# Memory updates in column tiles and memory reads in row tiles, with a new order of the work

## The chip, the cores and the metric

The kernel runs on one core of a Trainium2 chip. A core has TensorE (matmuls, "PE" in the profile, with its weight loads as "PEld"), VectorE ("DVE"), ScalarE ("ACT"), GpSimd ("POOL") and SyncE ("SP", which here issues nearly all DMAs). TensorE reads SBUF and writes PSUM, which has 8 banks; a bank holds 128 partitions x 512 floats. The metric is the device time of one execution in microseconds.

## The reference

Four layers work on x of 2048 tokens x 512 channels: attention with a compressive memory, a GEGLU feed-forward network, and both once more with the same weights. All inputs are bf16.

```python
x = x + A(layernorm(x));  x = x + B(layernorm(x))      # twice

def A(x):                       # 32 heads of 16 channels; 4 segments of 512 tokens
    q, k, v = split(x @ wq), split(x @ wk), split(x @ wv)
    phi = lambda t: where(t > 0, t + 1, exp(t))
    M, z = 0, 0                 # per head: 16 x 16 and 16
    for s in range(4):
        a_dot = softmax(qs @ ks.T / 4 + causal mask) @ vs
        a_mem = (phi(qs) @ M) / (phi(qs) @ z + 1e-6)
        o_s = sigmoid(beta) * a_mem + (1 - sigmoid(beta)) * a_dot
        M, z = M + phi(ks).T @ vs, z + sum(phi(ks))
    return concat(o) @ wo

def B(x):                       # 1792 hidden channels
    return (gelu(x @ w_gate) * (x @ w_up)) @ w_down
```

## The kernel before

**Stages.** The two attention layers with their four segments make eight attention segments, `Att(k)`, k = 0 to 7, and the two feed-forward layers eight `Ffn(k)`. Segment k of attention is followed by segment k of the feed-forward network; segments of different k overlap. Channels of q, k and v are in four blocks of 128 (b = 0 to 3), each with eight heads of 16 channels.

**TensorE's work.** Dense products (q, k, v, wo, gate, up, down) go through `product` (L399-409): a 128x128 weight tile against 512 columns. If the array is already split, the product is issued as four matmuls with 32 weight columns each ("columns", L406); otherwise as one ("whole", L409). Scores (`score_round`, L832) split the array by rows: four matmuls of four heads run beside each other ("rows"), each into another PSUM bank. `flush_item` (L848), which multiplies the exponentials with v, uses columns. `Clocks.tiling` marks each change between whole, rows and columns.

**The exponentials.** One ScalarE instruction (L1256) takes a pair of PSUM banks; GpSimd then zeroes the part above the diagonal (L1262). 320 such pairs make up the score work.

**The memory.** For every segment that is not the last of its layer, `upd_item` computes phi(k).T @ v: for each of four token tiles j and each block b one whole matmul of 128x128 weights with 128 columns (L758), 16 an update. Of the 128x128 results only the 16x16 blocks on the diagonal belong to a head, so VectorE masks them with `bd` into `mblk` (L770) and keeps a sum in `macc` (L785, L787); the sums z go into `zcols` (L774). The state is `mblk` (128 columns a block) and `zcols` (8 columns a block). For every segment that is not the first, `mem_items` reads it: 16 matmuls of 8 columns give the denominators (L681), VectorE adds the epsilon, multiplies with the gate and inverts (L688, L693), then for each block four matmuls of 128 columns give the numerators (L704), and VectorE scales one bank of 512 columns (L714) into `am`. `turn_later` has SP's queue transpose `am` into `amT` by DMA, and VectorE adds `amT` to the softmax part `aT` (L881). There are six updates and six reads in the program.

**What sets the order.** All five engines' instructions are written out by hand, in the order that `order` finds when the program is built: it keeps a clock for each engine, with a cost for each operation, and a list of `items` with due times, and at each step lets TensorE take score rounds first (`rounds_now`), then go on with an item that is open, then open the ready item that is due first, if a PSUM bank is free (`pick`). If nothing is ready while scores remain, TensorE multiplies a constant tile ("warm", a filler). Due times and slacks are in `POLICY`. The order is fixed in the program; on the chip the engines wait for each other by semaphores.

Of the kernel before, what the change touches and what calls it, by code (L numbers as in the profile page):

```python
# [18 lines left out]
P = 128  # L19
# [11 lines left out]
VW = H * (DH + 1)  # L31
SCALE = DH ** -0.5
# [12 lines left out]
def narrow(pieces, par):  # L45
# [19 lines left out]
    flush_wait=31.24, piece_slack=21.809, kb_slack=10.712, mem_slack=-1.256, margin=2.578, qk_due=1.366,  # L65
    e_q=-0.208, e_k=1.104, exp_slack=-8.673, e_slack=10.49, phi_slack=11.84, gelu_slack=-0.257, act_evict=7.504,
    first_evict=-5.126, gate_step=0.0, up_due=1.343, up_step=0.018, down_due=3.044, down_step=0.196,
    upd_due=-0.283, v0_due=-0.631, x1_at=2.428, x2_at=1.735, x3_at=6.651, x3_load=17.614, cut_slack=-5.505,
    direct=4, gelu_tiles=1, phi_pool=0, kb_dve=5, rounds=2, early=8.837, starve=0.645, ahead=0.994, near=-6.896,
    cap=1, soon=6.003)  # L70
# [187 lines left out]
def order(pol, nc, cst, seg, wrk, psp, A_x, A_wq, A_wk, A_wv, A_wo, A_beta, B_x, B_w_gate, B_w_up, B_w_down, out):  # L258
# [79 lines left out]
    maskB = cst.tile([P, 1], F32, name="maskB")  # L338
    nc.vector.reduce_sum(out=maskB[:], in_=bd[:, 16:P:32], axis=mybir.AxisListType.X)
# [4 lines left out]
    macc = cst.tile([P, 4, P], F32, name="macc")  # L344
# [11 lines left out]


    def later_constants():
        def column(va):
            nc.vector.tensor_copy(out=by_head(va)[:, :, :, DH], in_=cden[:].unsqueeze(1).to_broadcast([P, TPS, H]))  # L360
            nc.vector.memset(va[:, :, VW:], 0.0)

        for n, va in enumerate(vaugs[-1:] + vaugs[:-1]):
            ck.dve.post(12.0 + 3.0 * n, NORMAL, (0.4, lambda va=va: column(va), None))

# [148 lines left out]
    items = []  # L514
    e_jobs = []
# [4 lines left out]
    class Att:  # L520
# [12 lines left out]
        def add_items(self):  # L533
# [32 lines left out]
            def k_done(b, ps, at=None):  # L566
# [4 lines left out]
                def told(t):  # L571
# [5 lines left out]
                    if k < pol.kb_dve:  # L577
                        ck.dve.post(t, pol.kb_slack if k else NORMAL, (Slowed(0.345, 0.06), lambda: nc.vector.tensor_scalar(  # L578
                            out=self.kB[:, b, :], in0=self.kf[:, b, :], scalar1=maskB[:, 0:1], scalar2=None,
                            op0=ALU.mult), lambda t2: ev.update({("kB", k, b): t2})))  # L580
# [88 lines left out]
        def mem_items(self):  # L669
            k = self.k  # L670

            def ready(*more):
                return ck.has(*[("phiq", k, b) for b in range(4)], ("mem", k - 1), *more)

            den = Psum()

            def dens():
                return den()[:, 0:TPS * H].rearrange("p (j b h) -> p j b h", b=4, h=8)

            def den_mm(j, b):  # L680
                nc.tensor.matmul(dens()[:, j, b, :], lhsT=self.phiq[:, b, j * P:(j + 1) * P],  # L681
                                 rhs=mem_state[k - 1][1][:, b, :], start=True, stop=True)

            def den_done():
                def add():
                    self.rdm = wrk.tile([P, TPS, 4, 8], F32, tag="rdm", bufs=1, name="rdm")

                    nc.vector.scalar_tensor_tensor(  # L688
                        out=self.rdm[:], in0=dens(), scalar=EPS_MEM, op0=ALU.add, op1=ALU.mult,
                        in1=tmp_e2[:].rearrange("p (b h) -> p b h", h=8).unsqueeze(1).to_broadcast([P, TPS, 4, 8]))  # L690

                ck.dve.post(ck.made(), NORMAL, (0.273, add, den.read),
                            (0.956, lambda: nc.vector.reciprocal(out=self.rdm[:], in_=self.rdm[:]),  # L693
                             lambda t: ev.update({("den", k): t})))

            items.append(Item(k + 0.01, lambda: ready() and (self.s == 1 or ("am", k - 1) in ev),
                              [(Clocks.SMALL, whole(lambda j=j, b=b: den_mm(j, b))) for j in range(TPS) for b in range(4)],
                              den_done, kind="mem", ps=den, after=("phiq", k, 3)))

            def num(b):  # L700
                ps = Psum()

                def mm(j):
                    nc.tensor.matmul(ps()[:, j * P:(j + 1) * P], lhsT=self.phiq[:, b, j * P:(j + 1) * P],  # L704
                                     rhs=mem_state[k - 1][0][:, b, :], start=True, stop=True)

                def done():
                    self.n_num += 1
                    if self.n_num == 4:
                        ev["memn", k] = ck.pe  # L710

                    def scale():
                        self.am = seg.tile([P, TPS, P], BF16, tag=f"am{b % 2}", bufs=1, name="am")
                        nc.vector.tensor_tensor(  # L714
                            out=self.am[:].rearrange("p t (h e) -> p t h e", e=DH),
                            in0=ps()[:].rearrange("p (t h e) -> p t h e", h=8, e=DH),
                            in1=self.rdm[:, :, b, :].unsqueeze(3).to_broadcast([P, TPS, 8, DH]),
                            op=ALU.mult)

                    def told(t):  # L720
                        ps.read(t)
                        am = self.am
                        self.n_am += 1
                        if self.n_am == 4:
                            ev["am", k] = t
                        self.amT[b] = seg.tile([P, L], BF16, tag=f"amT{b}", bufs=1, name="amT")
                        turn_later(t, NORMAL, lambda: self.amT[b][:].rearrange("p (t q) -> p t q", q=P),
                                   lambda: am[:].rearrange("p t d -> p (t d)"),
                                   lambda t2: ck.at(t2 + 1.0, lambda: ev.update({("amT", k, b): t2 + 1.0})))

                    ck.dve.post(ck.made(), NORMAL, (0.683, scale, told))

                def go():
                    return (ready(("den", k)) and (b < 2 or ("amT", k, b - 2) in ev)
                            and (self.s == 1 or (("amT", k - 1, (b + 2) % 4 if b < 2 else b) in ev
                                                 and ("aT", k - 1, b) in ev)))

                return Item(k + 0.02 + 0.001 * b, go, [(Clocks.MM[128], whole(lambda j=j: mm(j))) for j in range(TPS)], done,
                            kind="mem", ps=ps, after=("den", k))

            for b in range(4):
                items.append(num(b))

        def upd_item(self):
# [3 lines left out]
            def blocks():  # L748
                return psm().rearrange("p (b d) -> p b d", d=P)
# [6 lines left out]
            def m(c):  # L756
                j, b = divmod(c, 4)
                nc.tensor.matmul(blocks()[:, b, :], lhsT=self.phik[:, j, b * P:(b + 1) * P],  # L758
                                 rhs=by_head(self.vaug)[:, j, 8 * b:8 * b + 8, 0:DH], start=(c == 0), stop=(c == n_mm - 1))

            def done():
# [3 lines left out]
                def kept(t):  # L765
                    made.append(seg.tile([P, 4, P], BF16, tag=f"mblk{k % 2}", bufs=1, name="mblk"))
                    made.append(seg.tile([P, 4, 8], BF16, tag=f"zcols{k % 2}", bufs=1, name="zcols"))

                def gated(src):
                    return lambda: nc.vector.tensor_tensor(out=made[0][:], in0=src(),  # L770
                                                           in1=bd[:].unsqueeze(1).to_broadcast([P, 4, P]), op=ALU.mult)

                def z():
                    nc.vector.tensor_tensor(out=made[1][:], in0=bd[:, 0:P:16].unsqueeze(1).to_broadcast([P, 4, 8]),  # L774
                                            in1=zacc[:].unsqueeze(2).to_broadcast([P, 4, 8]), op=ALU.mult)
# [5 lines left out]
                if self.s == 0:  # L781
                    steps = [(0.154, lambda: nc.vector.tensor_copy(out=zacc[:], in_=self.zk[:]), kept),
                             (0.683, gated(blocks), None),
                             (0.2, z, told),
                             (0.683, lambda: nc.vector.tensor_copy(out=macc[:], in_=blocks()), psm.read)]  # L785
                else:
                    steps = [(0.683, lambda: nc.vector.tensor_tensor(out=macc[:], in0=macc[:], in1=blocks(),  # L787
                                                                     op=ALU.add), psm.read),
                             (0.154, lambda: nc.vector.tensor_tensor(out=zacc[:], in0=zacc[:], in1=self.zk[:],
                                                                     op=ALU.add), kept),  # L790
                             (0.683, gated(lambda: macc[:]), None),
                             (0.2, z, told)]
                ck.dve.chain(ck.made(), pol.mem_slack, *steps)

            items.append(Item(k + pol.upd_due, ready, [(Clocks.MM[128], whole(lambda c=c: m(c))) for c in range(n_mm)],
# [406 lines left out]

    def open_item(got, bank):
# [85 lines left out]
    while streams or items or opened or ck.busy():  # L1289
        assert ck.pe < 2000.0, (streams[:1], [(it.kind, it.due) for it in items[:9]], e_jobs[:2], banks)  # L1290
        ck.serve()
        next_e()
# [92 lines left out]
```

## Time and profile before

| | before |
|---|---|
| median of 3 runs | 555.61 us (555.18 to 556.28) |
| span of the profiled execution | 553.5 us (first to last instruction; its device time as a whole isn't listed, the runs' times stand for it) |
| TensorE busy | 545.0 us, 98% |
| VectorE busy | 450.1 us, 81% |
| ScalarE busy | 445.3 us, 80% |
| GpSimd busy | 281.2 us, 51% |
| granted TensorE clock | 1.000 |

"Busy" of TensorE is the time in which some matmul is under way. Matmuls are pipelined, so a matmul's own duration is longer than the distance to the next. In the views of groups a row is: source line, engine, operation, out<-in, tile of the array and shapes, count, then busy time and mean duration in ns, then the engine's idle time before these instructions and what ended it. In the view of waits a row is: who waited, for whom, us in total, times, longest. The view in order of time has the start, the length and the group. Where a group of matmuls holds several shapes, the view in order of time names the first.

### The profile page before, as it was taken

How to read it: one execution, taken by the hardware profiler on the slowest of the kernel's cores; microseconds unless marked ns; L12 is line 12 of the kernel's file. 1: busy time of each engine (PE TensorE's matmuls, PEld its weight loads, DVE VectorE, ACT ScalarE, POOL GpSimd, SP SyncE). 2: the span in 40 equal slices, each digit the busy share in tenths (PEclk: the TensorE clock that was granted, in tenths of full speed). 3: DMA queues.
4: the chain of work that ended last, by engine and by line, in shares of the span. 5: the costliest groups of instructions: out<-in, count | busy, mean ns of one | idle time of the engine just before them, and what ended most of it. 6: DMA issues, size and time to landing. Idle time of an engine off the chain costs nothing.

```text
span 553.5 us, 22415 instructions
## 1 busy us (share of the span) xinstructions
PE 545.0 (98%) x9769; PEld 271.6 (49%) x9769; DVE 450.1 (81%) x837; ACT 445.3 (80%) x570; POOL 281.2 (51%) x410
## 2 busy tenths in 40 slices
PE   8999999999999999999999999999999999999997
PEld 4444554444544445444445445444554446455544
DVE  7999999879978999689896888968978696876062
ACT  5899999999999898999999899999539987930500
POOL 2687766268617878237882356836427264300000
PEclk9999999999999999999999999999999999999999
DMA  8246602500231032302142021031321006100001
GB/s 263 45 105 141 180 3 41 165 11 3 31 58 22 12 48 54 60 2 41 22 59 41 4 47 34 12 41 22 57 62 31 2 4 98 21 2 21 19 2 39
DMA packets 66467, 26.63 MB, mean 48 GB/s; under 512 B 55104, under 2 KB 66368, under 8 KB 66368
## 3 DMA queue, kind: packets, MB, share of 16 engines
q1 hardware_dynamic: 65936, 24.92, 21.7%
q8 instruction: 76, 1.25, 0.9%
q10 hardware_dynamic: 432, 0.27, 0.2%
q14 instruction: 23, 0.19, 0.1%
HBM read 9.71 MB, written 2.10 MB: 21 GB/s over the span
## 4 chain that ended last, share of the span: by engine, by line
PE 82%; DVE 13%; DMA 2%; issue 1%; ACT 0%; POOL 0%; DVEq 0%
PE ps L406 43%; PE ps L409 22%; PE ps L832 8%; PE ps L848 5%; DVE st L435 2%; DVE xn L465 1%; DVE byq L863 1%; DMA phik<-e 1%; DVE x_sb L918 1%; PE ps L704 1%; PE ps L758 1%; DVE vaug L396 1%; DVE q L396 1%; DVE ab L871 1%; DVE kB L578 1%
## 5 line engine op out<-in xcount | busy, mean ns | idle before, releaser
L1256 ACT ACTIVATE pt<-ps 128x1024 bf16<-128x1024 f32 x320 | 309.4, 1025 | 42.9 <-PE ps L832 32.5
L1262 POOL TENSOR_SCALAR_AFFINE_SELECT pt<-pt 128x512 bf16<-128x512 bf16 (+1 forms) x320 | 186.3, 589 | 182.2 <-ACT pt L1256 179.6
L978 DVE TENSOR_TENSOR gel_sb<-gel_sb,ps 128x512 bf16<-128x512 bf16 x112 | 76.4, 687 | 47.2 <-PE ps L406 27.8
L653 POOL TENSOR_SCALAR e<-e 128x512 bf16<-128x512 bf16 x48 | 74.2, 1546 | 4.7 <-ACT e L635 2.2
L406 PE MATMUL ps<-xnT,wu_sb 128*32 128x512 bf16 x1280 | 73.6, 379 | 0.0
L406 PE MATMUL ps<-xnT,wg_sb 128*32 128x512 bf16 x1144 | 68.9, 380 | 0.3 <-DVE x_sb L918 0.3
L918 DVE TENSOR_TENSOR x_sb<-x_sb,ps 128x512 bf16<-128x512 bf16 (+1 forms) x68 | 43.0, 643 | 24.6 <-PE ps L409 16.3
L406 PE MATMUL ps<-wd_sb,gel_sb 128*32 128x512 bf16 (+1 forms) x1060 | 60.5, 369 | 0.0
L863 DVE STREAM_TRANSPOSE byq<-ps 128x512 f32<-128x512 f32 x64 | 45.0, 705 | 6.7 <-PE ps L848 6.5
L406 PEld LDWEIGHTS <-wu_sb 128*32 128x32 bf16 x1280 | 33.0, 97 | 33.2 <-issue 2.8
L409 PE MATMUL ps<-wd_sb,gel_sb 128*128 128x512 bf16 (+1 forms) x239 | 45.1, 342 | 0.0
L406 PEld LDWEIGHTS <-wg_sb 128*32 128x32 bf16 x1144 | 28.9, 96 | 28.5 <-issue 5.5
L848 PE MATMUL ps<-pt,vaug 128*32 128x256 bf16 (+2 forms) x1568 | 40.8, 243 | 0.4 <-ACT gel_sb L956 0.3
L435 DVE BATCH_NORM_STATS2 st<-x_sb 128x6 f32<-128x512 bf16 x60 | 40.5, 674 | 0.2
L1030 ACT ACTIVATE gel_sb<-gel_sb 128x512 bf16<-128x512 bf16 x70 | 38.4, 628 | 0.1
L406 PEld LDWEIGHTS <-gel_sb 128*32 128x32 bf16 x1060 | 26.0, 96 | 24.1 <-issue 4.6
L409 PE MATMUL ps<-xnT,wg_sb 128*128 128x512 bf16 x162 | 37.7, 379 | 0.0
L848 PEld LDWEIGHTS <-vaug 128*32 128x32 bf16 x1568 | 31.9, 97 | 10.5 <-issue 2.9
L396 DVE CAST gel_sb<-ps 128x512 bf16<-128x512 f32 x46 | 30.8, 682 | 5.1 <-PE ps L406 4.7
L465 DVE TENSOR_SCALAR xn<-x_sb,mv,rs 128x512 bf16<-128x512 bf16 x64 | 30.7, 534 | 1.2 <-POOL rs L453 0.9
L832 PE MATMUL ps<-q,kf 16*128 16x256 bf16 (+1 forms) x896 | 31.1, 232 | 0.2 <-DVE vaug L396 0.2
L409 PEld LDWEIGHTS <-gel_sb 128*128 128x128 bf16 x239 | 22.6, 98 | 17.0
(129 smaller groups left out, 739.0 us busy)
## 6 DMA issues: line engine op xcount, KB each, us to landing
wg_sb<-in_B_w_gate_dram SPq DMA_DIRECT2D x8, 224.0 KB, 3.6
wu_sb<-in_B_w_up_dram SPq DMA_DIRECT2D x8, 224.0 KB, 4.6
wd_sb<-in_B_w_down_dram SPq DMA_DIRECT2D x7, 256.0 KB, 3.2
x_sb<-in_A_x_dram SPq DMA_DIRECT2D x3, 512.0 KB, 8.0
out_dram<-x_sb SPq DMA_DIRECT2D x12, 128.0 KB, 1.8
xnT<-xn SPq DMA_TRANSPOSE x48, 2.5
kB<-kf SPq DMA_DIRECT2D x48, 16.0 KB, 1.8
wv_sb<-in_A_wv_dram SPq DMA_DIRECT2D x1, 512.0 KB, 7.1
```

Source lines behind the costliest of these rows:

```text
L396: ck.dve.post(ck.made(), slack, (0.673, lambda: nc.vector.tensor_copy(out=dst(), in_=src()), end), taken=taken)
L406: nc.tensor.matmul(out[r], lhsT=lhsT[:, r], rhs=rhs, start=start, stop=stop, tile_position=(0, 32 * c))
L409: nc.tensor.matmul(out, lhsT=lhsT, rhs=rhs, start=start, stop=stop)
L435: nc.vector.bn_stats(out=self.st6[:, 0, :], in_=x_sb[:, self.tt0 + j, :])
L653: return lambda: eng.tensor_scalar(out=e[0][:], in0=e[0][:], scalar1=1.0, scalar2=None, op0=ALU.min)
L832: nc.tensor.matmul(ps_all[:, pair[unit // 2], o:o + n], lhsT=lhsT[rows, b, P * ki:P * ki + P], rhs=self.q[rows, b, q0:q0 + n], start=True, ...
L848: nc.tensor.matmul(ps()[32 * j:32 * j + 32, q0:q0 + n], lhsT=self.vaug[:, ki, h * (DH + 1):h * (DH + 1) + 32], rhs=pt_all[:, slot, unit, c ...
L863: nc.vector.transpose(out=self.byq[:, par, :, :].rearrange("p a c -> p (a c)"), in_=ps()[:])
L918: ck.dve.post(ck.made(), slack, (0.15 + 0.00104 * (c1 - c0), lambda: nc.vector.tensor_tensor(out=xt, in0=xt, in1=ps()[:, 0:c1 - c0], op=AL ...
L978: ck.dve.post(ck.made(), NORMAL, (0.683, lambda: nc.vector.tensor_tensor(out=g, in0=g, in1=ps()[:], op=ALU.mult), lambda t: (ps.read(t), e ...
L1256: nc.scalar.activation(out=pt_all[:, s0, :, :].rearrange("p (h u) c -> p h (u c)", h=2), in_=ps_all[:, p0[0]:p0[1] + 1, :], func=ACT.Exp, ...
L1262: nc.gpsimd.affine_select(out=half, in_=half, pattern=[[0, w], [1, P]], compare_op=ALU.is_ge, fill=0.0, base=0, channel_multiplier=-1)
```

## The change

The state of the memory becomes one tile `mz` with 34 columns a block: two heads of 16 columns and one column of z each. The update is issued in four column tiles: for each token tile and block four matmuls with 32 weight columns (two heads) and 32 columns of v. So each result has only 32 columns, of which two 16x16 blocks are kept, and VectorE's steps on it have 128 elements in place of 512. The read is issued in four row tiles: 32 rows of phi(q) (two heads) against 34 columns of `mz`, into four banks, denominators beside numerators. It works on half of the blocks at a time (`mem_event`), as a single block of 32 matmuls, and no longer through `items`: `mem_now` starts it when its inputs are there and two pairs of banks are free. VectorE then has per half two additions (32 elements), one reciprocal (64) and four scalings (256), with the gate laid out in a new constant `e2x`. The values of `POLICY` are others, so that the whole order of the work is new; `kb_dve` goes from 5 to 4 (the copy kB of the keys is made by DMA for one more segment) and `direct` from 4 to 5 (one more of each segment's 14 gate tiles goes through GELU straight from PSUM).

```diff
+MZ = 2 * DH + 2
 POLICY = dict(
-    flush_wait=31.24, piece_slack=21.809, ..., kb_dve=5, ..., direct=4, ...)
+    flush_wait=152.105, piece_slack=40.738, ..., kb_dve=4, ..., direct=5, ..., am_slack=1.081, mem_wait=0.156)
...
-    maskB = cst.tile([P, 1], F32, name="maskB")
-    nc.vector.reduce_sum(out=maskB[:], in_=bd[:, 16:P:32], axis=mybir.AxisListType.X)
+    mask2 = cst.tile([P, 2 * DH], F32, name="mask2")
+    nc.vector.reduce_sum(out=mask2[:], in_=bd[:].rearrange("p (c n) -> p n c", c=4), axis=mybir.AxisListType.X)
...
-    macc = cst.tile([P, 4, P], F32, name="macc")
+    macc = cst.tile([P, 4, 2 * DH], F32, name="macc")
+    e2x = cst.tile([P, 2, 2, 2, 4 * TPS], F32, name="e2x")
...
         def mem_items(self):
-            ...  (den_mm, den_done, num: one item for the denominators, four for the numerators)
+            for half in range(2):
+                mem_jobs.append((self.k + 0.01 + 0.002 * half, self, half))
+
+        def mem_event(self, half, pairs):
+            k, bs = self.k, (2 * half, 2 * half + 1)
+            ck.tiling("rows")
+            mz = mem_state[k - 1][0]
+            for n in range(2 * TPS):
+                b, j = bs[n // TPS], n % TPS
+                for g in range(4):
+                    r = slice(32 * g, 32 * g + 32)
+                    nc.tensor.matmul(ps_all[:, pairs[g // 2][g % 2], MZ * n:MZ * (n + 1)],
+                                     lhsT=self.phiq[r, b, j * P:(j + 1) * P], rhs=mz[r, b, :], start=True, stop=True,
+                                     tile_position=(32 * g, 0))
+            ...
+            ck.dve.post(ck.made(), pol.am_slack, (0.16, add(0), None), (0.16, add(1), None), (0.52, inverse, None),
+                        (0.78, scale(0), lambda t: read(0, t)), (0.78, scale(1), told))
...
         def upd_item(self):
             def m(c):
                 j, b = divmod(c, 4)
-                nc.tensor.matmul(blocks()[:, b, :], lhsT=self.phik[:, j, b * P:(b + 1) * P],
-                                 rhs=by_head(self.vaug)[:, j, 8 * b:8 * b + 8, 0:DH], start=(c == 0), stop=(c == n_mm - 1))
+                ck.tiling("columns")
+                for g in range(4):
+                    r = slice(32 * g, 32 * g + 32)
+                    nc.tensor.matmul(blocks()[r, b, :], lhsT=self.phik[:, j, b * P + 32 * g:b * P + 32 * g + 32],
+                                     rhs=by_head(self.vaug)[:, j, 8 * b + 2 * g:8 * b + 2 * g + 2, 0:DH], start=(c == 0),
+                                     stop=(c == n_mm - 1), tile_position=(0, 32 * g))
...
+    def mem_now():
+        if not mem_jobs or len(free_pairs()) < 2:
+            return False
+        got = [j for j in mem_jobs if j[1].mem_ready(j[2])]
+        ...
+        job[1].mem_event(job[2], pairs)
+        return True
...
         ck.serve()
         next_e()
+        if mem_now():
+            continue
         n = rounds_now()
```

More of the change, by code (lines that the diff above doesn't have):

```diff
@@ L64 @@
 POLICY = dict(
[L65 to L70, printed above, removed]
+    flush_wait=152.105, piece_slack=40.738, kb_slack=10.905, mem_slack=-2.348, margin=2.56, qk_due=0.594,
+    e_q=-0.77, e_k=1.073, exp_slack=-18.49, e_slack=11.096, phi_slack=6.459, gelu_slack=-0.034, act_evict=5.372,
+    first_evict=-0.382, gate_step=0.0, up_due=1.256, up_step=0.012, down_due=3.948, down_step=1.013,
+    upd_due=-0.62, v0_due=1.254, x1_at=0.158, x2_at=5.744, x3_at=0.964, x3_load=17.129, cut_slack=-0.231,
+    direct=5, gelu_tiles=1, phi_pool=0, kb_dve=4, rounds=2, early=0.939, starve=0.658, ahead=0.286, near=-3.652,
+    cap=7, soon=1.448, am_slack=1.081, mem_wait=0.156)
 class Slowed(float):
@@ L355, in gate_constants, with gate_rows @@
         nc.vector.tensor_scalar(out=tmp_e2[:], in0=tmp_e2[:], scalar1=1.0, scalar2=None, op0=ALU.add)
+    def gate_rows(half, b):
+        for p in range(2):
+            nc.vector.tensor_copy(
+                out=e2x[:, half, p, :, 2 * TPS * b:2 * TPS * (b + 1)].rearrange("p g (j h) -> p g j h", h=2),
+                in_=tmp_e2[:].rearrange("p (a b q g h) -> p a b q g h", a=2, b=2, q=2, g=2)[:, half, b, p, :, :]
+                .unsqueeze(2).to_broadcast([P, 2, TPS, 2]))
     def later_constants():
@@ L364, in later_constants @@
             ck.dve.post(12.0 + 3.0 * n, NORMAL, (0.4, lambda va=va: column(va), None))
+        for n in range(4):
+            ck.dve.post(26.0 + 2.0 * n, NORMAL, (0.25, lambda n=n: gate_rows(*divmod(n, 2)), None))
     def turn_later(t, slack, out, in_, landed, margin=0.0):
@@ L669, in mem_items @@
         def mem_items(self):
[L670 to L739, printed above, removed]
@@ L741, in mem_items, with mem_ready @@
-            for b in range(4):
-                items.append(num(b))
+            for half in range(2):
+                mem_jobs.append((self.k + 0.01 + 0.002 * half, self, half))
+        def mem_ready(self, half):
+            k, s, bs = self.k, self.s, (2 * half, 2 * half + 1)
+            return (ck.has(*[("phiq", k, b) for b in bs], by=ck.pe - 0.055) and ck.has(("mem", k - 1), by=ck.pe - 0.055)
+                    and (s == 1 or all(("amT", k - 1, b) in ev and ("aT", k - 1, b) in ev for b in bs)))
@@ L1201, in pick @@
         return min(got, key=lambda i: (-len(pairs_of(set(range(BANKS)) - {i, *apart})), banks[i]))
+    def mem_now():
+        if not mem_jobs or len(free_pairs()) < 2:
+            return False
+        got = [j for j in mem_jobs if j[1].mem_ready(j[2])]
+        if not got or (ck.mode != "rows" and streams and min(got)[0] > streams[0][0] + streams[0][1] / STEPS + pol.mem_wait):
+            return False
+        job = min(got, key=lambda j: j[0])
+        mem_jobs.remove(job)
+        pairs = sorted(free_pairs(), key=lambda p: max(banks[p[0]], banks[p[1]]))[:2]
+        job[1].mem_event(job[2], pairs)
+        return True
     def open_item(got, bank):
@@ L1287, in order @@
     owner = defaultdict(list)
-    while streams or items or opened or ck.busy():
+    while streams or items or mem_jobs or opened or ck.busy():
         assert ck.pe < 2000.0, (streams[:1], [(it.kind, it.due) for it in items[:9]], e_jobs[:2], banks)
```

75 lines of the change are left out of this document (59 added, 16 removed).

## The prediction

> **What bounds the kernel now.** I read the page first (span, busy shares, chain), then the waits, then stretches of the span, then TensorE's instructions in order of time, because a busy share cannot say what one instruction costs.
>
> ```profile
> span 553.5 us, 22415 instructions
> PE 545.0 (98%) x9769; PEld 271.6 (49%) x9769; DVE 450.1 (81%) x837; ACT 445.3 (80%) x570; POOL 281.2 (51%) x410
> ...
> PE 82%; DVE 13%; DMA 2%; issue 1%; ACT 0%; POOL 0%; DVEq 0%
> ```
> ```profile
> 28.00:165.00 137.00, 134.61 (x2510) 66.44 (x2510) 126.04 (x237) 129.34 (x164) 88.38 (x123) 1.00 0.33 74
> 165.00:390.00 225.00, 224.08 (x4420) 109.19 (x4421) 192.07 (x349) 210.23 (x265) 139.12 (x195) 1.00 0.19 32
> ...
> 490.00:553.50 63.50, 59.99 (x540) 31.20 (x532) 28.71 (x51) 9.55 (x16) 1.27 (x2) 1.00 0.06 18
> ```
> In the second fence the columns are: stretch, its length, then busy time of PE, PEld, DVE, ACT and POOL, the granted clock, and the DMA's share and rate. TensorE is busy everywhere, at full clock. ScalarE is close behind it until 390 us (129.3 of 137, 210.2 of 225) and has nearly nothing to do at the end. So a microsecond of TensorE work taken out should come off the span, unless ScalarE or a full PSUM then makes TensorE wait. What TensorE waits for today is little:
>
> ```profile
> PE ps L758 <- DMA phik<-e: 1.0, 2, 0.6
> ...
> PE ps L409 <- DVE am L714: 0.5, 1, 0.5
> ```
>
> Matmuls overlap, so their mean duration is not their price. The price is the distance from one start to the next. Here are starts in order of time (start, length of the group, group):
>
> ```profile
> 10.28 0.40 PE L832 MATMUL ps<-wd_sb 16*128 16x256 bf16 x8
> 10.61 1.04 PE L409 MATMUL ps<-xnT,wq_sb 128*128 128x512 bf16 x4
> ...
> 12.22 0.41 PE L832 MATMUL ps<-wd_sb 16*128 16x256 bf16 x20
> 12.56 0.39 PE L409 MATMUL ps<-xnT,wk_sb 128*128 128x512 bf16 x1
> ```
> ```profile
> 143.62 0.56 PE L681 MATMUL ps<-zcols,phiq 128*128 128x8 bf16 x16
> 144.03 1.02 PE L409 MATMUL ps<-xnT,wg_sb 128*128 128x512 bf16 x4
> ...
> 145.32 1.90 PE L409 MATMUL ps<-xnT,wg_sb 128*128 128x512 bf16 x8
> 147.06 0.61 PE L704 MATMUL ps<-mblk,phiq 128*128 128x128 bf16 x8
> 147.51 1.67 PE L409 MATMUL ps<-xnT,wg_sb 128*128 128x512 bf16 x7
> ```
> ```profile
> 189.25 0.96 PE L758 MATMUL ps<-vaug,phik 128*128 128x128 bf16 x13 [0.61 <-DMA phik<-e]
> 190.05 1.02 PE L409 MATMUL ps<-xnT,wq_sb 128*128 128x512 bf16 x4
> ```
> ```profile
> 149.98 1.70 PE L406 MATMUL ps<-xnT,wg_sb 128*32 128x512 bf16 x28
> 151.60 0.40 PE L832 MATMUL ps<-q,kB 32*128 32x256 bf16 x8
> 151.93 1.69 PE L406 MATMUL ps<-xnT,wg_sb 128*32 128x512 bf16 x28
> ```
> - A whole 512-column matmul takes (147.06 - 145.32)/8 = 0.217 us. Seven sets of four column tiles take 151.60 - 149.98 = 1.62 us, which is 7 x 0.216 and 0.11 more. So four tiles together cost what one whole matmul costs, and a change of tiling costs about 0.1 us.
> - Two sets of four row tiles with 256 columns, with the change behind them, take 10.61 - 10.28 = 0.33 us. One such set and four sets of 64 columns (the third and fourth piece of a score round at L832) take 12.56 - 12.22 = 0.34 us. A set of 256 takes (0.33 - 0.10)/2 = 0.115 us, so a set of 64 takes (0.34 - 0.10 - 0.115)/4 = 0.03 us for all four of its matmuls.
> - The denominators take 0.41/16 = 0.0256 us each, the 128-column reads 0.45/8 = 0.056, the 128-column updates 0.80/13 = 0.0615.
>
> **The change, part by part.**
>
> ```profile
> L704 PE MATMUL ps<-mblk,phiq 128*128 128x128 bf16 x96 | 7.9, 220 | 0.0
> ...
> L758 PE MATMUL ps<-vaug,phik 128*128 128x128 bf16 x80 | 6.4, 224 | 1.0 <-DMA phik<-e 1.0
> ...
> L406 PE MATMUL ps<-warm 128*32 128x512 bf16 x72 | 4.7, 381 | 0.0
> ...
> L758 PE MATMUL ps<-gel_sb,phik 128*128 128x128 bf16 x16 | 1.3, 224 | 0.0
> ...
> L681 PE MATMUL ps<-zcols,phiq 128*128 128x8 bf16 x96 | 3.3, 167 | 0.0
> L409 PE MATMUL ps<-warm 128*128 128x512 bf16 x7 | 1.8, 380 | 0.0
> ```
> *Removed from TensorE:* 96 denominators x 0.0256 = 2.5 us, 96 reads x 0.056 = 5.4 us, 96 updates x 0.0615 = 5.9 us: 13.8 us, all on the path.
>
> *Added to TensorE:* 384 update matmuls of 32 columns are 96 sets of four column tiles, 384 reads of 34 columns are 96 sets of four row tiles. No row shows such a short set. Nearest is the set of 64 columns at 0.03 us, with the same weight loads. Below it lies 34/64 of it, 0.016, if only columns count. Above it I put a whole 128-column matmul, 0.056, if loading or issue of the many small instructions sets the pace (an update is 64 loads and 64 matmuls on end, more than any run of short sets before). I take 0.03, because the loads stay and columns are few: 192 x 0.03 = 5.8 us. Ends: 3.1 and 10.8 us.
>
> The Trainium skill, TensorEngine Tiling (Array Packing), section "Instruction Overhead", speaks against the change: a matmul has an overhead of about 60 cycles, so one with a single column lasts as long as one with 60, and a tiling factor should not be taken from a dimension that is already small. For 8 whole columns the trace agrees with a floor (0.0256 us). But the 0.03 us for four tiled matmuls shows that the four share it. By the rule paid by every matmul the sum would be the first rival's 562 us, by the row it is the forecast below.
>
> *New order.* The same dense products, scores and flushes stand in both programs. Counted in the program's order, the fillers in the score stages are 72/4 + 7 = 25 before, 76/4 + 9 = 28 after: 3 x 0.216 = +0.65 us. The changes of tiling are 350 and 351: +0.1 us. They only change in kind: 106 to or from whole matmuls become 74, direct ones between rows and columns go from 244 to 277, and both cost 0.1 us. The work after the last flush is as long as before (both 69.5 us by these prices), so the end does not change its nature; it is whole dense work that neither ScalarE nor VectorE holds up.
>
> *VectorE* (81%, off the path by the chain except 13%):
>
> ```profile
> L396 DVE CAST gel_sb<-ps 128x512 bf16<-128x512 f32 x46 | 30.8, 682 | 5.1 <-PE ps L406 4.7
> ...
> L714 DVE TENSOR_TENSOR am<-ps,rdm 128x512 bf16<-128x512 f32 x24 | 15.6, 681 | 0.0
> ...
> L867 DVE RECIPROCAL r<-byq 128x32 f32<-128x32 f32 x32 | 11.3, 354 | 1.1
> ...
> L693 DVE RECIPROCAL rdm<-rdm 128x128 f32<-128x128 f32 x6 | 5.7, 953 | 0.2
> L918 DVE TENSOR_TENSOR x_sb<-x_sb,ps 128x256 bf16<-128x256 bf16 x8 | 3.4, 420 | 5.4 <-PE ps L409 4.1 <-PE ps L406 1.4
> ...
> L688 DVE SCALAR_TENSOR_TENSOR rdm<-ps,tmp_e 128x128 f32<-128x128 f32 x6 | 1.6, 273 | 0.0
> ...
> L774 DVE TENSOR_TENSOR zcols<-bd,zacc 128x32 bf16<-128x32 f32 x6 | 1.2, 204 | 0.0
> ```
> A read of one segment was 0.273 + 0.953 + 4 x 0.681 = 3.95 us. It becomes two halves, each 2 small adds (0.2, the 32-element row), a reciprocal of 64 (0.55, a third of the way from 0.354 for 32 to 0.953 for 128) and four scalings of 256 elements (0.42): 2.6 us a half, so 6 x (5.2 - 3.95) = +7.6 us over six segments. An update's two 512-element steps of 0.68 become 128-element ones of 0.27: 6 x 2 x -0.41 = -4.9 us. By the order VectorE also loses 11 evictions of gel_sb, gains 8 small constants, and makes 4 fewer kB copies: about -8 us. Together -5 us; I cost it at nothing, since TensorE's own work covers it.
>
> *ScalarE* takes those 11 evictions (it loses 7 GELU passes and some others): about +1 us, hidden beside TensorE. *SP's queue* gets 16 more kB transfers of 16 KB (64 for 48), issued between the transposes of xnT and amT; each holds whatever transpose stands behind it, but their takers are a segment away, so I cost it at nothing. If that cover goes, the next scores with kB are late. *Waits:* a read now is one block of 32 matmuls needing four free banks at once, and scores, flushes and dense products share the other four until VectorE has read them; before, a read took one bank at a time. I take the price as nothing, from the one such wait of today, 0.5 us; the upper end is the second rival. The last scores run in order behind it, so a wait there would be passed on to everything.
>
> *Sum.* 553.5 - 13.8 + 5.8 + 0.65 + 0.1 = 546.3 us of span, which is -7.2 us. The median of the runs is 555.6, some 2.1 above the span of the profiled execution (launch and end, and spread of runs). So I forecast 555.6 - 7.2 = **548.4 us**. With the ends for the new sets: 545.7 to 553.4 us. Less than nothing is possible too: the wait on am (0.5) and that on phik (1.0) may go, down to about 544.
>
> **The rivals.**
> - *Each small tiled matmul pays its own floor* (ends slower). At 0.0256 us each, the row of the denominators, 768 matmuls take 19.7 us in place of 13.8: 555.6 + 5.9 + 0.75 = 562.2 us. It decides from 0.068 us a set on. For it: an unbroken run of 128 instructions has no row. Against it: 0.03 us for four matmuls of 64 columns.
> - *A read takes PSUM away.* VectorE needs 2.6 us behind whatever it has to do, and four banks are shut so long. If each of the 12 halves costs TensorE what the wait on am costs now and a little more, 0.6 us, the gain of 7.2 us is gone: 555.6 us, no change; above 0.6 us it is slower. For it: ScalarE waits for scores now.
>
> ```profile
> ACT pt L1256 <- PE ps L832: 32.5, 40, 15.5
> ```
> That wait is mostly the tail of the program and the few places where scores come late, and the program puts dense products into free banks right behind the reads I looked at (banks 6 and 7 while 2 to 5 are held). Against it too: two of the four banks come free 0.8 us before the others, when the first pair of scalings is done.
> - *ScalarE keeps the pace.* Until 390 us it is 94% busy (339.6 of 362 us). If the time TensorE saves there only turns into waiting for exponentials, of the gain only the part behind 390 us is left, about a third: 555.6 - 2.4 = 553.2 us. The three extra fillers are a first sign; against it, after the scores are done 69.5 us of dense work remain that can be pulled forward.
>
> **How the numbers follow.** Forecast 0.78 (own range 545.7 to 551.5), each pays its floor 0.05 (562), PSUM 0.10 (553 to 558), ScalarE 0.07 (553). The least that a measurement of this kernel can tell from no change is about 0.2%, 1.1 us. Faster holds the forecast, ScalarE and a third of PSUM: 0.88. Same is a third of PSUM, 0.03. Slower is the floor and the rest of PSUM: 0.09. The range goes from 545.0, the forecast with its waits gone in part, to 553.5, which takes in ScalarE's case and the 0.056 us end; the floor and most of PSUM stay outside.
>
> **What would show it.** In the profile after: a read of 32 matmuls starts and the next group follows 0.24 us plus one change of tiling later, an update of 64 matmuls 0.48 us; TensorE still about 98% busy; the same full clock. If the floor rules, a read takes 0.8 us. If PSUM does, there are waits of TensorE on VectorE's am behind the reads, and idle time in the table of waits well above today's. If ScalarE does, its busy share before 390 us goes to 97% and TensorE has gaps at the scores. What would make me wrong most: a new wait in the new order that its instruction counts do not show, such as a transposed phik or amT that lands late.

## The result, and the profile after

The changed kernel takes **547.65 us** (median of 4 runs, 547.49 to 548.11), 0.986 of the kernel before (95% interval 0.9845 to 0.9874). Of a before of 555.6 us that is 7.8 us (7.0 to 8.6). 548.4 us was forecast, within 545.0 to 553.5. One more execution of the kernel before, a slow one of 616.92 us, is not in the 555.61 us of the table.

The page of the changed kernel, its parts on span, busy time and the chain:

```profile
span 546.1 us, 23526 instructions
PE 535.6 (98%) x10291; PEld 266.0 (49%) x10321; DVE 442.4 (81%) x880; ACT 445.5 (82%) x572; POOL 278.8 (51%) x410
...
PE 83%; DVE 12%; issue 2%; DMA 2%; ACT 0%; DVEq 0%
```

The span is 7.4 us shorter, TensorE's busy time 9.4 us. Busy shares are what they were, but for ScalarE's 82% in place of 80%, whose time grew by 0.2 us; VectorE lost 7.7 us. (30 of TensorE's matmul records are missing from this trace, 10291 against 10321 weight loads, all of them at L421. The 1.7 us of TensorE's "issue" gaps at L421 in the next view are most likely these, so that some 1.7 of the 9.4 us may be missing records.) The waits of TensorE in the changed kernel: who waited, for whom, us in total, times, longest.

```profile
PE ps L421 <- issue: 1.7, 11, 0.2
PE ps L320 <- DVE warm L313: 1.1, 1, 1.1
PE ps L769 <- DMA phik<-e: 0.8, 2, 0.5
PE ps L507 <- DVE q L408: 0.8, 1, 0.8
...
PE ps L421 <- DVE am L730: 0.3, 1, 0.3
```

The two waits shown before the change are still there, and a little shorter: phik 0.8 us for 1.0, am 0.3 for 0.5. So the new order has no new large wait. What changed is the price of the memory's matmuls. TensorE's work in order of time (start, length, group), a read, two pieces of an update, and a whole update:

```profile
152.29 0.37 PE L700 MATMUL ps<-mz,phiq 32*128 32x34 bf16 x32
152.59 3.20 PE L418 MATMUL ps<-xnT,wg_sb 128*32 128x512 bf16 x56
```
```profile
123.97 0.27 PE L769 MATMUL ps<-vaug,phik 128*32 128x32 bf16 x16
124.17 0.40 PE L848 MATMUL ps<-q,kB 32*128 32x256 bf16 x8
124.50 0.53 PE L769 MATMUL ps<-vaug,phik 128*32 128x32 bf16 x48
124.86 1.06 PE L418 MATMUL ps<-wo_sb,aT 128*32 128x512 bf16 x16
```
```profile
376.87 0.69 PE L769 MATMUL ps<-vaug,phik 128*32 128x32 bf16 x64
377.47 0.83 PE L418 MATMUL ps<-xnT,wq_sb 128*32 128x512 bf16 x12
```

A read of half a segment starts at 152.29, the next group 0.30 us later: without the 0.1 us for the change of tiling, 0.20/8 = 0.025 us for a set of four. An update's 12 sets take 124.86 - 124.50 = 0.36 us, 0.030 a set, its other 4 sets 0.20 us with a change, 0.025. So 96 x 0.025 + 96 x 0.029 = 5.2 us stand where 13.8 us stood. These pieces are the cheap ones: the update in the last rows takes 377.47 - 376.87 = 0.60 us for its 16 sets, 0.037 a set, and with that price for all updates the sum would be 6.0 us. VectorE's new steps:

```profile
L730 DVE TENSOR_TENSOR am<-ps,rdm 128x256 bf16<-128x256 f32 x48 | 17.0, 416 | 0.4
L724 DVE RECIPROCAL rdm<-rdm 128x64 f32<-128x64 f32 x12 | 6.6, 553 | 0.4
L718 DVE SCALAR_TENSOR_TENSOR rdm<-ps,e2x 128x32 f32<-128x32 f32 x24 | 3.3, 176 | 0.2 <-PE ps L700 0.2
...
L803 DVE TENSOR_TENSOR macc<-macc,ps 128x128 f32<-128x128 f32 x4 | 1.1, 265 | 0.0
```

Forecast were 0.42, 0.55, 0.2 and 0.27 us.

### The profile page after: what moved, and what is told of

Read it like the earlier page. It is cut to its first block, busy times and chain, and to the rows that moved or that the text cites. A ratio compares the mean times of both kernels' runs of the same rounds, so it can differ in the third digit from the quotient of the medians.

```text
span 546.1 us, 23526 instructions
## 1 busy us (share of the span) xinstructions
PE 535.6 (98%) x10291; PEld 266.0 (49%) x10321; DVE 442.4 (81%) x880; ACT 445.5 (82%) x572; POOL 278.8 (51%) x410
## 4 chain that ended last, share of the span: by engine, by line
PE 83%; DVE 12%; issue 2%; DMA 2%; ACT 0%; DVEq 0%
PE ps L418 45%; PE ps L421 21%; PE ps L848 8%; PE ps L864 6%; DVE st L447 1%; DMA phik<-e 1%; DVE byq L879 1%; PE ps L320 1%; DVE x_sb L934 1%; DVE xn L477 1%; DVE ab L887 1%; DMA xnT<-xn 1%; DVE e L652 1%; PE ps L700 1%; DVE gel_sb L408 1%
## 5 line engine op out<-in xcount | busy, mean ns | idle before, releaser
L418 PE MATMUL ps<-wd_sb,gel_sb 128*32 128x512 bf16 (+1 forms) x1452 | 81.5, 364 | 0.0
L418 PE MATMUL ps<-xnT,wg_sb 128*32 128x512 bf16 x1040 | 63.3, 380 | 0.2 <-DVE gel_sb L408 0.2
L418 PE MATMUL ps<-xnT,wu_sb 128*32 128x512 bf16 x956 | 55.3, 380 | 0.0
L418 PEld LDWEIGHTS <-gel_sb 128*32 128x32 bf16 x1452 | 35.9, 96 | 31.3 <-issue 6.5
L421 PE MATMUL ps<-xnT,wu_sb 128*128 128x512 bf16 x202 | 45.9, 379 | 0.7 <-issue 0.3
L421 PE MATMUL ps<-xnT,wg_sb 128*128 128x512 bf16 x178 | 40.9, 379 | 1.0 <-issue 0.5
L418 PEld LDWEIGHTS <-wu_sb 128*32 128x32 bf16 x956 | 24.3, 97 | 25.1 <-issue 2.6
L1046 ACT ACTIVATE gel_sb<-gel_sb 128x512 bf16<-128x512 bf16 x63 | 35.0, 632 | 0.0
L418 PE MATMUL ps<-wo_sb,aT 128*32 128x512 bf16 x500 | 31.3, 380 | 0.2 <-DVE x_sb L934 0.2
L421 PEld LDWEIGHTS <-wu_sb 128*128 128x128 bf16 x209 | 19.9, 98 | 23.6 <-issue 0.2
```

What stands on the lines that cost most here:

```text
L418: nc.tensor.matmul(out[r], lhsT=lhsT[:, r], rhs=rhs, start=start, stop=stop, tile_position=(0, 32 * c))
L421: nc.tensor.matmul(out, lhsT=lhsT, rhs=rhs, start=start, stop=stop)
```

## The experiments

The first theory is that the gain is TensorE's shorter list of instructions, and that all other work fits behind it. Its rivals are a floor that each small matmul pays for itself, PSUM banks, ScalarE's pace, and the new order as such. All the times below are medians beside runs of the kernel before on the same chip; the ratios are to that. A difference to the changed kernel is the difference of the ratios times 555.6 us; by the intervals of both ratios it is known to about 1.2 us (1.8 us for the reads issued three times over).

### What a set costs: reads three times over, and sorted by tile

```diff
-            for n in range(2 * TPS):
+            for n in 3 * list(range(2 * TPS)):
```


> The changed kernel with every read of the memory issued three times into the same banks, in the same order of everything else (the result is unchanged). It adds 192 sets of four row tiles with 34 columns on TensorE. If the span follows TensorE's instructions, each costs 0.025 to 0.03 us and the time is 547.65 + 4.8 to 5.8 = 552.5 to 553.4 us (0.994 to 0.9955 of before). If something else sets the pace there and TensorE has slack, it stays at 547.7 us.

Measured: 557.97 us, 1.0038 (1.0010 to 1.0066): 9.9 us more than the changed kernel, about twice what was expected.

```diff
-            for n in range(2 * TPS):
-                b, j = bs[n // TPS], n % TPS
-                for g in range(4):
+            for g in range(4):
+                for n in range(2 * TPS):
+                    b, j = bs[n // TPS], n % TPS
```


> The changed kernel with the 32 matmuls of a read sorted by row tile: eight on tile 0, then eight on tile 1 and so on, so that neighbours are no longer on different tiles. The same instructions and the same result. If four small matmuls share a floor only because they stand beside each other on four tiles, each now pays about 0.0256 us: a read takes 32 x 0.0256 = 0.82 us in place of about 0.22, and the time is 547.65 + 12 x 0.6 = 554.8 us. If sharing does not depend on the order, it stays at 547.7 us.

Measured: 550.56 us, 0.9918 (0.9903 to 0.9933): 3.2 us more, neither 7 nor 0.

The same read in order of time, first issued three times over, then sorted by tile:

```profile
154.10 0.92 PE L700 MATMUL ps<-mz,phiq 32*128 32x34 bf16 x96
154.95 3.21 PE L418 MATMUL ps<-xnT,wg_sb 128*32 128x512 bf16 x56
```
```profile
153.20 0.73 PE L700 MATMUL ps<-mz,phiq 32*128 32x34 bf16 x32
153.85 3.20 PE L418 MATMUL ps<-xnT,wg_sb 128*32 128x512 bf16 x56
```

Three reads on end take 0.85 us, 0.10 of it for the change: 0.75/24 = 0.031 us a set, dearer than the 0.025 of a short read, so a long run of short sets does not keep the short run's pace. By that the 12 reads cost 12 x (0.85 - 0.30) = 6.6 us more. In the profiled run another 1.8 us is a single gap behind a read, ended by nothing that the profile shows (TensorE's "issue"):

```profile
PE ps L421 <- issue: 1.8, 1, 1.8
```
```profile
293.10 1.06 PE L700 MATMUL ps<-mz,phiq 32*128 32x34 bf16 x96
295.93 4.45 PE L421 MATMUL ps<-xnT,wg_sb 128*128 128x512 bf16 x12 [1.77 <-issue]
300.21 0.59 PE L421 MATMUL ps<-xnT,wu_sb 128*128 128x512 bf16 x2
```

And the stretch around it, with the granted clock third from the end:

```profile
290.00:300.00 10.00, 8.15 (x184) 4.03 (x177) 6.39 (x19) 5.96 (x11) 2.65 (x2) 0.84 0.50 75
```

The twelve matmuls behind the gap take 300.21 - 295.93 = 4.28 us, where 12 x 0.217 = 2.6 us are usual: 1.7 us more, at a granted clock of 0.84 in these 10 us. So 6.6 + 1.8 + 1.7 = 10.1 us account for the 9.9. What made the gap and the lower clock is open. Two of the six runs have a mean clock of 0.999 in place of 0.997 and took 556.3 and 556.8 us, still 2 us or more above 547.65 + 6.6; no profile shows where theirs went.

Sorted by tile, 32 matmuls take 0.65 - 0.10 = 0.55 us: 0.017 us each, against 0.025/4 = 0.006 with neighbours on four tiles. So the four matmuls of a set overlap only when they stand beside each other on four tiles. On one row tile each pays 0.017 us, not the 0.0256 of an 8-column matmul on the whole array. Whether 0.017 is a floor isn't shown: at the pace of the 512-column matmul, 34 columns alone would take 0.217 x 34/512 = 0.014 us. 12 x (0.65 - 0.30) = 4.2 us were to be expected from the trace, 3.2 were measured, within the intervals. That each small matmul pays for itself, as the first rival has it, does happen, then, at a smaller price, and this kernel avoids it by its order of loops.

### ScalarE's pace

```diff
                     nc.scalar.activation(out=e[0][:], in_=src, func=ACT.Exp)
+                    if which == "k":
+                        nc.scalar.activation(out=e[0][:, 0:P], in_=src[:, 0:P], func=ACT.Exp)
```


> The changed kernel with 24 more exponentials of 128 columns on ScalarE, one behind each exponential for phi(k) (same result): 24 x 0.22 to 0.3 = 5 to 7 us more ScalarE work, nearly all before 400 us. If ScalarE sets the pace of the score stages, most of it shows: 552 to 554 us. If TensorE does, 547.7 to 549 us.

Measured: 547.99 us, 0.9872 (0.9857 to 0.9887): 0.7 us more, which the intervals do not tell from nothing; they allow up to 1.8. ScalarE's busy time went from 445.5 to 451.0 us, nearly all before 400 us (364.5 to 369.4). So at most a third of the added work shows, and ScalarE does not set the pace, although in the changed kernel it is 96% busy from 28 to 165 us (131.42 of 137).

### PSUM or VectorE: the scalings twice, and extra work beside the banks

```diff
-                    for g in range(2):
+                    for g in (0, 1, 0, 1):
                         c = 2 * DH * (2 * p + g)
```


> The changed kernel with VectorE's four scalings of each half of a read done twice over (same result). VectorE has 12 x 4 x 0.42 = 20 us more work, and the four banks of a read stay shut 0.84 us (first pair) and 1.7 us (second pair) longer, without the order knowing it. If TensorE's own instructions set the span, TensorE finds other banks and the time stays below 550 us. If the banks held by a read are what limits, each of the 12 halves costs 0.84 to 1.7 us: 558 to 568 us.

Measured: 557.86 us, 1.0050 (1.0036 to 1.0065): 10.6 us more, at the lower end of what the banks were to cost. VectorE's busy time is 14.4 us longer (456.8), not 20. TensorE's waits for a read's banks in this run:

```profile
PE ps L848 <- DVE am L730: 1.1, 5, 0.3
PE ps L421 <- DVE am L730: 0.6, 1, 0.6
PE ps L864 <- DVE am L730: 0.6, 1, 0.6
PE ps L700 <- DVE am L730: 0.5, 2, 0.4
```

They are 2.8 us, against 0.3 in the changed kernel: there, but a part only. And the run does not separate the banks from VectorE's own lateness. The next one puts the work where it holds no bank of its read:

```diff
+                    for g in (0, 1, 0, 1) if p else ():
+                        nc.vector.tensor_tensor(
+                            out=spare_out[:], in0=spare_in[:],
+                            in1=rdm()[:, p, g, :]...to_broadcast([P, 2 * TPS, 2, DH]), op=ALU.mult)
```


> The changed kernel with 48 more VectorE products of the size of a scaling, from SBUF to SBUF, behind the last scaling of each half of a read (same result): VectorE has 17 to 20 us more, as in the run with the scalings done twice, but the four banks come free as early as in the changed kernel. If the banks made the 10 us of that run, this one is at 547.7 to 550 us; if VectorE's lateness did, at 555 to 558 us.

Measured: 563.03 us, 1.0150 (1.0133 to 1.0166): 16.1 us more, although the extra work stands behind the scalings that free a read's banks. TensorE's busy time, VectorE's, and TensorE's waits in this run:

```profile
PE 541.0 (96%) x10321; PEld 267.3 (48%) x10321; DVE 462.2 (82%) x928; ACT 446.2 (80%) x572; POOL 279.1 (50%) x411
```
```profile
PE ps L856 <- DVE gel_sb L411: 2.3, 2, 1.5
PE ps L424 <- DVE gel_sb L1002: 1.9, 2, 1.0
PE ps L421 <- DVE gel_sb L411: 1.7, 2, 1.5
PE ps L856 <- DVE byq L887: 1.6, 2, 1.2
PE ps L703 <- DVE gel_sb L411: 1.3, 1, 1.3
```

19.8 us more of VectorE work make the kernel 16.1 us slower, 0.81 us for each; with the scalings done twice it was 10.6 for 14.4, 0.74 for each. TensorE waits for work that has nothing to do with the memory: evictions of gate results (L411), the products of the feed-forward network (L1002), the flushes' transposes (L887). All of these read PSUM, so TensorE waits for banks here too, but for those of other work that VectorE comes to late; for `am` it waits 0.6 us. So VectorE's lateness suffices for such a loss, without the read's own banks.

### The update whole again, and its two halves

```diff
-                for g in range(4):
-                    r = slice(32 * g, 32 * g + 32)
-                    nc.tensor.matmul(blocks()[r, b, :], ..., tile_position=(0, 32 * g))
+                nc.tensor.matmul(blocks()[:, b, :], lhsT=self.phik[:, j, b * P:(b + 1) * P],
+                                 rhs=by_head(self.vaug)[:, j, 8 * b:8 * b + 8, 0:DH], ...)
...
+                def strips(fn):
+                    for g in range(4):
+                        fn(slice(32 * g, 32 * g + 32))
```


> The changed kernel, order kept, with the update's 16 matmuls whole again (128 weight columns, 128 columns of v, 0.0615 us each) and the state built by VectorE from the 32 columns that count, in four strips of 32 partitions. TensorE has 96 x (0.0615 - 0.028) = 3.2 us more, and some changes of tiling more; VectorE some 10 us more. If the gain is TensorE's instructions, the time is about 551 us, 0.991 to 0.993 of before. If the gain is the new order, it stays at 547.7 us.

Measured: 561.43 us, 1.0113 (1.0095 to 1.0131): 14.1 us more. I had expected 3.3, and VectorE's strips to be covered. The two halves of the edit, one at a time:

```diff
-                for g in range(4): ...
+                nc.tensor.matmul(psm()[:, b * P:(b + 1) * P], ...)
-                return psm()[:, 0:4 * 2 * DH].rearrange("p (b d) -> p b d", d=2 * DH)
+                return psm().rearrange("p (b d) -> p b d", d=P)[:, :, 0:2 * DH]
```


> The changed kernel, order kept, with the update's 16 matmuls whole again on TensorE, but VectorE's steps left as they are in number and size: they read 32 columns of each block, which are the right ones for a quarter of the partitions only, so the state of the memory is left incomplete. TensorE has 96 x (0.0615 - 0.028) = 3.2 us more, VectorE nothing. If TensorE's instructions carry the loss that the whole update with VectorE's strips showed (13.8 us), it comes back here; if VectorE's strips do, the time is 551 us (0.991 to 0.993).

Measured: 549.35 us, 0.9897 (0.9880 to 0.9913): 2.1 us more, near the 3.2 expected, which the two intervals together just allow.

```diff
-                    return lambda: nc.vector.tensor_tensor(out=heads()[:, :, :, 0:DH], ...)
+                    return lambda: strips(lambda r: nc.vector.tensor_tensor(out=heads()[r, :, :, 0:DH], ...))
```


> The changed kernel with TensorE's work as it is and VectorE's steps on the update cut into four strips of 32 partitions (same result). A strip takes about 0.28 us like the whole step, so VectorE has 36 x 0.28 = 10 us more, which the order does not know of. If the loss of the whole update with strips came from VectorE being late in a fixed order: 556 to 558 us. If TensorE alone counts: below 549 us.

Measured: 559.48 us, 1.0081 (1.0066 to 1.0096): 12.3 us more, from 12.4 us of VectorE work. The strips of the update and TensorE's waits in this run:

```profile
L788 DVE TENSOR_TENSOR mz<-macc,mask 32x128 bf16<-32x128 f32 x16 | 5.3, 334 | 0.3
L810 DVE TENSOR_TENSOR macc<-macc,ps 32x128 f32<-32x128 f32 x16 | 4.5, 279 | 0.3
```
```profile
PE ps L418 <- DVE x_sb L941: 2.4, 2, 1.3
PE ps L855 <- DVE byq L886: 2.3, 2, 1.3
PE ps L418 <- DVE macc L808: 2.0, 1, 2.0
```

A strip of 32 partitions takes as long as the whole step of 128 (0.279 us for 0.265). The halves add up: 2.1 + 12.3 = 14.4 us, for the 14.1 measured together. TensorE's part agrees with its price within the intervals; VectorE's comes out in full.

### The read whole again

```diff
-MZ = 2 * DH + 2
+MZ = 8 * (DH + 1)
...
-                for g in range(4): ...
+                nc.tensor.matmul(ps_all[:, pairs[n // 4][n // 2 % 2], MZ * (n % 2):MZ * (n % 2 + 1)],
+                                 lhsT=self.phiq[:, b, j * P:(j + 1) * P], rhs=mz[:, b, :], start=True, stop=True)
```


> The changed kernel, order kept, with the read's sets replaced by whole matmuls of 128 rows against 136 columns (eight heads with their denominators, a block-diagonal state), 8 in a half: 96 x (0.062 - 0.027) = 3.4 us more on TensorE, and up to 1 us for changes of tiling. VectorE's steps on the products have the same sizes. If the gain is TensorE's instructions: 551 to 552 us. If it is the new order or the merging of denominators and numerators: 547.7 us.

Measured: 552.26 us, 0.9949 (0.9934 to 0.9964): 4.9 us more, where 3.4 to 4.4 were expected. VectorE's busy time is 5.7 us longer (448.1), since the state's masking is now four steps for one, and by the runs above that costs too. A read in this run, between the same kinds of neighbours as the one shown of the changed kernel:

```profile
153.58 0.65 PE L698 MATMUL ps<-mz,phiq 128*128 128x136 bf16 x8
154.16 1.05 PE L418 MATMUL ps<-xnT,wg_sb 128*32 128x512 bf16 x16
```

It takes 0.58 us for 0.30, so 12 reads at most 12 x 0.28 = 3.4 us more. The row tiles of the read are worth at most 4.9 us, then, and by TensorE's rows up to 3.4; the rest fits VectorE's longer work, but wasn't separated from it. This run keeps the denominators beside the numerators; the read of the kernel before, with both apart, was not put back.

### The order alone, and the tiles alone

```diff
-    flush_wait=152.105, piece_slack=40.738, ..., direct=5, ..., cap=7, soon=1.448, am_slack=1.081, mem_wait=0.156)
+    flush_wait=31.24, piece_slack=21.809, ..., direct=4, ..., cap=1, soon=6.003, am_slack=1.081, mem_wait=0.156)
```


> The changed kernel's tiles with the values that set the order taken from the kernel before (the two new ones kept). In its order of instructions are 92 fillers of 512 columns, where the changed kernel has 28: 64 x 0.216 = 13.8 us more on TensorE. If the span follows TensorE's instructions: 561.5 us, 1.010 of before, so that the tiles without an order made for them lose. If the tiles carry the gain by themselves: below 550 us.

Measured: 565.20 us, 1.0189 (1.0172 to 1.0206).

```diff
-    flush_wait=31.24, piece_slack=21.809, ..., direct=4, ..., cap=1, soon=6.003)
+    flush_wait=152.105, piece_slack=40.738, ..., direct=5, ..., cap=7, soon=1.448, am_slack=1.081, mem_wait=0.156)
```


> The kernel before with the values that set the order taken from the changed kernel: the memory whole as before, the order new. Its order has 33 fillers where before has 25, and 353 changes of tiling where before has 350: 8 x 0.216 + 0.3 = 2.0 us more on TensorE. If the span follows TensorE's instructions: about 557.7 us (1.0036). If the new order carries the gain: about 548 us.

Measured: 559.81 us, 1.0085 (1.0070 to 1.0100).

Either half of the change alone is slower than the kernel before: the tiles in an order made for the old work by 1.9%, the new order with the old work by 0.85%. In both the fillers in the list of instructions pointed the right way, and by the ratios 4.5 and 2.7 us came on top that the list does not show. Waits are the likely place, but they were not added up. In the second run VectorE's busy time is 437.4 us, 12.7 less than before, and the kernel is slower all the same, so less VectorE work brought no gain by itself. The gain belongs to TensorE's shorter work only together with an order that was made for it; neither is a cause by itself. No run searches a fresh order for the old tiles, so what a fresh search alone would give is not known.

### VectorE's extra work in an order that knows it

```diff
-                        (0.78, scale(0), lambda t: read(0, t)), (0.78, scale(1), told))
+                        (0.78, scale(0), lambda t: read(0, t)), (0.78, scale(1), told),
+                        (1.62, more, None))
...
-    flush_wait=152.105, piece_slack=40.738, ..., kb_dve=4, ..., direct=5, ...)
+    flush_wait=165.61, piece_slack=32.129, ..., kb_dve=8, ..., direct=6, ...)
```


> The 48 extra VectorE products of the run before, in an order made with them: their cost stands in the step list of a read, behind the scalings, and the values of POLICY were searched anew. TensorE's list is as short as in the changed kernel (29 fillers against 28, 349 changes of tiling against 351), so by its instructions alone the time is that of the changed kernel, 547.5 us, 548 to 550 with some more waits. If VectorE's total work limits the span whatever the order, 20 us more on it keep the time at 555 to 563 us.

Measured: 555.51 us, 0.9987 (0.9973 to 1.0002): 7.1 us more than the changed kernel, 9.1 less than the same extra work in the order that did not know of it. So the forecast by TensorE's list fails, and the time lies at the lower end of the other one. TensorE's list is as long as in the changed kernel by its fillers and changes of tiling. The busy times, and the longest of TensorE's waits that are longer than in the changed kernel:

```profile
PE 541.5 (98%) x10454; PEld 268.3 (49%) x10454; DVE 460.8 (83%) x927; ACT 450.6 (81%) x582; POOL 282.1 (51%) x411
```
```profile
PE ps L779 <- DMA phik<-e: 1.3, 3, 0.6
...
PE ps L702 <- DVE phiq L654: 0.7, 2, 0.3
PE ps L858 <- DVE kf L410: 0.7, 1, 0.7
PE ps L702 <- DVE x_sb L944: 0.6, 2, 0.4
```

These waits are short, on DMA and VectorE both, and do not add up to 7 us: TensorE's idle time is 553.2 - 541.5 = 11.7 us, for 546.1 - 535.6 = 10.5 in the changed kernel (8.8 without the 1.7 of missing records). So 1.2 to 2.9 of the 7 us are idle time, and the rest lies in TensorE's busy time, where this view does not tell who is waited for. The new values of POLICY also move other work (ScalarE has 5.1 us more). So about half of the cost of VectorE's extra work went with an order made for it; that the other half is waiting for VectorE is not shown, nor whether a better order would remove it.

## Why the prediction was right

- *Removed, 13.8 us:* the rows before gave it; the update's half, put back on TensorE alone, cost 2.1 us (3.2 by the rows, which the intervals just allow). The read's half rests on the rows, since the old read was not put back.
- *Added, 192 sets at 0.03 us = 5.8 us:* they measured 0.025 (reads) and 0.029 to 0.037 (updates), 5.2 to 6.0 us. The row of the 64-column sets was the right neighbour, and the ends of 0.016 and 0.056 were not reached. My reason for the upper end, many instructions on end, exists in small: at 24 sets on end a set of a read costs 0.031 us.
- *Fillers and changes of tiling, +0.75 us:* counted, and not contradicted: by the measured prices 13.8 - 0.75 less 5.2 to 6.0 is 7.1 to 7.9 us; the span fell by 7.4 us and the time by 7.8.
- *Waits at nothing:* right in this order (am 0.3 us, phik 0.8 us). The step was argued from too little, though: an instruction list does not show waits, and in the two runs with only half of the change 2.7 and 4.5 us came on top of what the list said.
- *VectorE at nothing, "since TensorE's own work covers it":* the result did not contradict it, because VectorE's work fell (-7.7 us measured, -5 forecast), but the reason was wrong. TensorE's work does not cover VectorE: 12.4 us more on it cost 12.3 us in the fixed order, and 18.4 us more went with 7.1 us in an order made with them. A VectorE that is 81% busy, with 12% of the chain, has hardly any slack in the fixed order. If the change had added that much to VectorE, the forecast would have failed; in this term the forecast was lucky. How much of the gain the 7.7 us saved on VectorE made possible wasn't separated; in the run with the old tiles in the new order 12.7 us less brought none.
- *ScalarE at nothing:* shown, 5.5 us more on it cost 0.7 us (at most 1.8). Its rival is out, though from 28 to 165 us ScalarE is busier than VectorE (131.42 us for 125.17).
- *The rival on the floor:* small matmuls do pay one by one (0.017 us each, not 0.0256) when neighbours share a row tile. It does not apply, because the loops put four tiles beside each other.
- *The rival on PSUM:* the scalings done twice, which hold the read's banks longer, cost 10.6 us for 14.4 us of VectorE work; work beside those banks cost 16.1 for 19.8. The read's banks weren't needed for the loss. A share of theirs isn't excluded, since TensorE's waits for `am` were 2.8 us in the first of these runs. In the changed kernel they are 0.3 us.

## What to carry to other kernels

Price a matmul by the distance between starts, and a set of tiles by the nearest set that the trace holds; keep the four tiles next to each other in the list. Where the order of all engines is fixed in the program, an engine's busy share says little about its slack: ask with a run what a few microseconds more on it cost, since here 81% on VectorE meant hardly any slack and 82% on ScalarE meant enough for 5.5 us. And a change of work and the order made for it are to be judged together: each alone lost here.

## What had not been expected of the hardware

Four row-tile matmuls of 34 columns on four tiles start 0.025 us after the four before them (8 sets on end), and 0.031 us in a run of 24 sets. Eight on end on one row tile take 0.017 us each, less than the 0.0256 us of an 8-column matmul on the whole array. VectorE takes as long for 32 partitions as for 128 (0.279 and 0.265 us for 128 elements).
